# Sliding-window attention and a tanh-shrink feed-forward layer: a new order of loads in the first batch, another form of the second, and another V product in the third and fourth

## Chip, core and metric

The kernel runs on one core of a Trainium2 chip. The metric is the device time of one execution in microseconds; the time of a kernel is the median of its runs. The core has five engines, each with its own queue of instructions worked off in order: TensorE (matrix products), VectorE, ScalarE, GpSimd and SyncE. Transfers are issued from the queues of SyncE, ScalarE and GpSimd.

## What is computed

Eight batches of eight heads, 576 positions, head dimension 64. Each query attends to itself and the 63 positions before it. The attention output, 4608 tokens of 512 values, goes through a feed-forward layer with 2048 hidden values. Everything comes in and goes out as float32; the kernel works in bfloat16 with float32 accumulation.

```python
scores = scale * np.matmul(q, k.transpose(0, 1, 3, 2))
rel = pos[:, None] - pos[None, :]
scores = np.where((rel >= 0) & (rel < 64), scores, -1e9)
attn = softmax(scores)
x = (attn @ v).transpose(0, 2, 1, 3).reshape(B * S, H * D)
h = x @ w_in
out = (h - np.tanh(h)) @ w_out
```

## The kernel before

**Tiling.** Two heads (h and h + 4 of a batch) form a pair; pair g belongs to batch g // 4, so there are 32. The 576 positions are nine windows of 64. The keys of a window lie on 128 partitions (64 earlier ones and its own 64), so a score tile is 128 keys by 64 queries for each head. The feed-forward layer works on nine chunks of 512 tokens (eight windows); a chunk has 16 hidden tiles (`h`, four matmuls each, then tanh on ScalarE and the subtraction L392 on VectorE) and 16 output groups (`y`, four matmuls each; after every fourth, `y_out` copies a 128-row result out of PSUM and stores it).

**One pair of heads.** `load` brings q and k of a pair, cast to bfloat16 on the way, by a transfer issued on GpSimd; the tiles `kall` and `qall` hold a whole batch and there are two of each. Then q and k are transposed on TensorE, in one of two ways. `tr_heads` (L255) transposes straight from the loaded layout, 12 small transposes for six row groups and two heads. `cast` first rearranges on an engine to `qb` or `kb`, and `tr` (L263) then needs six; it copies q out twice, one half by ScalarE, one by VectorE (`qt`, zero-padded, both heads in one product). Scores follow, an exponential on ScalarE writes `pt`, and keys outside the window must be made nothing. This is done in two ways too. `hides` (L281) puts a large negative bias into PSUM by two matmuls ahead of the scores. Or the exponentials are multiplied on VectorE by a mask of zeros and ones (L300, L327), which lies in PSUM bank 5, written there once by `see`.

**V.** `load_v_all` brings a batch of V (`vall`, one buffer), `cast_v` rearranges it to `vb` with a column of ones, and nine transfers make the windows `vw`: `keys_v` writes the upper 64 partitions, and `shift_dve` makes the lower ones by copies on VectorE (batches 0 and 1); `windows_v` writes both by transfer (batch 2 from GpSimd, the later ones from SyncE). The product of probabilities and V carries the sum of the probabilities in the column of ones. `tile_pv` (L309) makes it with 20 matmuls of 64 columns of the array each, the two heads side by side, and normalizes by one reciprocal (L313) and one product on 128 partitions (L315). `pv` and `norm` make it with nine matmuls over both heads (L333), one reciprocal (L340) and two products on 64 partitions (L344). `x_tr` (L350) transposes the result to the tokens' chunk `xT`.

**Order.** The schedule is written out by hand. The instructions of batch 0 come first, straight in line. Then comes a list of positions h: `OPS[h]` says which hidden tile or output group TensorE does at h, and `at(h, ...)` hangs the attention work of later batches behind it. Positions 0 to 30 (even) are chunk 0's hidden tiles, 32 to 47 its output groups, 48 to 63 chunk 1's hidden tiles, 64 to 79 its output groups, and so on. Batch 1 hangs at 33 to 47, pairs 8 to 11 at 50 to 77 and pairs 12 to 15 at 68 to 94 (by `std`, whose product with V is `whole_pv`). PSUM has eight banks; the numbers in the calls are banks. In the first batch scores go to banks 0, 1 and 4, 5; hidden tiles of chunks 0 to 2 use banks 0 to 2, the output groups of chunks 0 and 1 banks 1 and 2.

**What the steps below touch.** GpSimd's queue takes its loads, V's moves and its casts in the written order. Pairs 8, 9 and 12 to 14 have their casts on VectorE, pairs 10, 11 and 15 on GpSimd. Before the change pair 10's q is cast at position 55 and its k at 56, pair 11's at 60 and 61, and the loads of pairs 12 to 15 are issued at 60 and 61.

Of the kernel before, what the change touches and what calls it, by code (L numbers as in the profile page):

```python
# [8 lines left out]
BF16 = mybir.dt.bfloat16  # L9
ALU = mybir.AluOpType  # L10
# [5 lines left out]
def kernel(  # L16
# [9 lines left out]
    nc = tc.nc  # L26
    B, H, S, D = q.shape
    NP = H // 2
# [29 lines left out]
    ident = const.tile([128, 128], BF16, name="ident")  # L58
    tick = const.tile([1, 1], BF16, name="tick")
    seen = const.tile([128, 128], BF16, name="seen")  # L60
    mask = ps[:, 5, 448:480].bitcast(BF16)
    hide = const.tile([128, 2, 64], BF16, name="hide")
    WIDE = 1024, 1024
# [17 lines left out]
    def move(eng, o, i):  # L81
        if eng is nc.scalar:
            nc.scalar.activation(o, i, ACT.Copy)  # L83
        else:
            eng.tensor_copy(o, i)  # L85

    def load(g, n, eng):

        b, pr = divmod(g, NP)
        if g == 0:  # L90
            t = qk_pool.tile([P, 2, E * D], F32, tag=n, name=n + "f")
        else:
            if (b, n) not in whole:
                whole[b, n] = all_pool.tile([P, H, E * D], BF16, tag=n, name=n + "all")
            t = whole[b, n][:, pr::NP]
        eng.dma_start(out=t, in_=(q if n == "q" else k)[b, pr::NP].rearrange("h (p e) d -> p h (e d)", e=E))  # L96
        stage[g, n] = t
# [8 lines left out]
    def pace(h):  # L106

        c, m = divmod(h // 2 - 1, M)
        nc.gpsimd.tensor_copy(tick, gT[c][0:1, m, 0:1])
# [101 lines left out]
    def make_seen():  # L211
# [2 lines left out]
        nc.gpsimd.affine_select(seen, seen, compare_op=ALU.is_ge, fill=0.0,  # L214
                                base=64, pattern=[[-1, 128]], channel_multiplier=1)

    def see():
        nc.tensor.transpose(ps[:, 5, 448:512].bitcast(BF16), seen, ident)

# [55 lines left out]

    GROUPS = (0, 5), (5, 4)

    def hides(grp, banks):
        n = GROUPS[grp][1]
        for h in range(2):  # L280
            nc.tensor.matmul(ps[:, banks[h], 0:64 * n], ident, hide[:, h].unsqueeze(1).to_broadcast([128, n, 64]),  # L281
                             start=True, stop=False)

    def tile_scores(g, grp, banks, how="hide"):

        j0, n = GROUPS[grp]
        if how == "hide":
            hides(grp, banks)
        for i in range(n):
            j = j0 + i  # L290
            for h in range(2):
                r = slice(64 * h, 64 * h + 64)
                nc.tensor.matmul(ps[:, banks[h], 64 * i:64 * i + 64], kT[g % NR][r, 64 * j:64 * j + 128],  # L293
                                 qs[g % 2][r, 64 * j:64 * j + 64], start=how == "mask", stop=how == "mask" or i == n - 1)
        o = PT[g % NPT][:, j0:j0 + n].rearrange("p j (h t) -> p h j t", h=2)
        nc.scalar.activation(o, pair_of(banks)[:, :, 0:64 * n].rearrange("p h (j t) -> p h j t", t=64),  # L296
                             ACT.Exp, scale=scale)
        if how == "mask":
            p = PT[g % NPT][:, j0:j0 + n].rearrange("p j (h t) -> p (j h) t", h=2)
            nc.vector.tensor_tensor(p, p, mask.unsqueeze(1).to_broadcast([128, 2 * n, 64]), ALU.mult)  # L300

    def tile_pv(g, banks):

# [123 lines left out]
    def at(h, fn, *args):  # L427
        items.setdefault(h, []).append((fn, args))

    def pace(h):  # L430

        c, m = [OPS[i][1:] for i in range(h) if OPS.get(i, "-")[0] == "h"][-1]
        nc.gpsimd.tensor_copy(tick, gT[c][0:1, m, 0:1])
# [13 lines left out]
    load(1, "q", G)  # L447
    make_hide()
    make_seen()
    load(2, "k", G)  # L450
    load(2, "q", G)

    warm(9)
    cast_flat(0, "q", V)
# [3 lines left out]
    see()  # L458
    for pr in range(NP):
        cast_v(0, pr, V)  # L460
    tile_scores(0, 0, (0, 1))
    tile_scores(0, 1, (4, 5))
    for j, eng in enumerate((Y, G, A, G, Y, G, G, Y, G)):
        keys_v(0, j, eng)
    for n in "kq":
        load(3, n, G)
    load_w_in(0)
    load_w_in(1)
    load_w_out(0)
# [10 lines left out]
    tile_scores(1, 0, (0, 1), "mask")  # L480
    tile_scores(1, 1, (4, 5), "mask")
    tr_heads(2, "q", 3, A)
    tile_scores(2, 0, (0, 1), "mask")
    tile_scores(2, 1, (4, 5), "mask")
    tr_heads(3, "k", 2, V)
    shift_dve(0, 0, 4)
    tile_pv(0, (6, 7))
    tr_heads(3, "q", 3, A)
    hides(0, (0, 1))
    hides(1, (4, 5))  # L490
    tile_scores(3, 0, (0, 1), "hidden")
    tile_scores(3, 1, (4, 5), "hidden")
    tile_pv(1, (6, 7))
    tile_pv(2, (2, 3))
    tile_pv(3, (0, 1))
    x_tr(0, 0, 0, 4, 4, A)
    x_tr(0, 0, 4, 9, 5, A)
    warm(2)
    x_tr(0, 1, 0, 4, 6, V)
    x_tr(0, 1, 4, 9, 3, A)  # L500

    at(33, lambda: [cast_v(1, pr, V) for pr in range(NP)])
    at(34, more_constants)
    at(35, lambda: [keys_v(1, j, G) for j in range(NJ)])
    at(35, load, 7, "q", G)
    at(35, load_v_all, 2)
    for g in 8, 9:
        at(35, load, g, "k", G)
        at(35, load, g, "q", G)
    at(39, tr_heads, 4, "k", 3, V)  # L510
    at(40, tr_heads, 4, "q", 0, A)
    at(41, tile_scores, 4, 0, (4, 5))
    at(41, tr_heads, 5, "k", 3, V)
    at(42, tile_scores, 4, 1, (4, 5))
    at(42, tr_heads, 5, "q", 0, A)
    at(43, tile_scores, 5, 0, (4, 5))
    at(43, tr_heads, 6, "k", 3, V)
    at(44, tile_scores, 5, 1, (4, 5))
    at(44, tr_heads, 6, "q", 0, A)
    at(45, tile_scores, 6, 0, (4, 5))  # L520
    at(45, shift_dve, 1, 0, 4)
    at(46, tile_scores, 6, 1, (4, 5))
    at(46, tr_heads, 7, "k", 3, V)
    at(46, tr_heads, 7, "q", 0, A)
    at(46, tile_pv, 4, (6, 7))
    at(47, tile_scores, 7, 0, (4, 5))
    at(47, tile_pv, 5, (6, 7))
    at(47, tile_scores, 7, 1, (4, 5))
    at(47, x_tr, 1, 0, 0, 4, 3, V)
    at(47, tile_pv, 6, (6, 7))  # L530
    at(47, x_tr, 1, 0, 4, 9, 0, A)
    at(47, tile_pv, 7, (4, 5))
    at(47, x_tr, 1, 1, 0, 4, 3, V)
    at(47, x_tr, 1, 1, 4, 9, 6, A)

    at(48, lambda: [cast_v(2, pr, G) for pr in range(NP)])
    at(49, lambda: [windows_v(2, j, G) for j in range(NJ)])
    for g in 10, 11:
        at(49, load, g, "k", G)
        at(49, load, g, "q", G)  # L540
    at(49, load_v_all, 3)
    for g in range(12, 16):
        at(60 + (g - 12) // 2, load, g, "k", G)
        at(60 + (g - 12) // 2, load, g, "q", G)
    for i in range(2):
        at(140 + 4 * i, more_zeros, i)

    def whole_pv(g):
        for i in range(3):
            pv(g, i)  # L550
        norm(g)

    def std(g, ck, cq, t, tk, ss, ms, p):
        at(cq, cast, g, "q", V if g not in (10, 11, 15) else G)
        at(ck, cast, g, "k", V if g not in (10, 11, 15) else G)
        at(t, tr, g, "q", 3, A, V)
        at(tk, tr, g, "k", 3, A)
        for i in range(3):
            at(ss + 2 * i, scores, g, i, 4)
        at(ms, masking, g)  # L560
        at(p, whole_pv, g)

    for i, g in enumerate(range(8, 12)):
        a = (50, 55, 60, 65)[i]
# [63 lines left out]
                    at(h, pace, h)  # L628
                    at(h, *f)

    done = None
    for h in range(32 * NC + 32):
        op = OPS.get(h)
        if op and done:
            y_out(*done)
            done = None
        if op and op[0] == "h":
            c, m = op[1:]
            if c < 2 and m == 0:
                hp_mm(c, (0, 1, 2), True)  # L640
            elif c > 1 or m > 2:
                hp_mm(c, (m,), False)
        elif op:
            yp_mm(*op[1:])
            if op[2] % 4 == 3:
                done = op[1], op[2] // 4
# [4 lines left out]
    y_out(*done)  # L651
    assert not items

# [28 lines left out]
```

The softmax here doesn't subtract the row's maximum and nothing guards it: scores larger than these inputs give would overflow.

## Time and profile before

| | us |
|---|---|
| median of 4 runs (349.55 to 351.45) | 349.84 |
| the profiled execution | 349.65 |
| its span, first to last instruction | 347.9 |
| TensorE matmul busy in the span | 319.2 (92%) |
| VectorE busy | 200.5 (58%) |
| ScalarE busy | 184.8 (53%) |
| GpSimd busy | 110.5 (32%) |

Busy times are unions of the intervals in which an engine had an instruction under way. They are averages over stages with different limits, so the stages have to be read one by one. The granted clock of TensorE is a share of full speed; its mean over the span is 0.974. The profile names the tile that an instruction writes and those that it reads ("kall<-in_k_dram" is a load of k), and the line that recorded it; L85 and L83 are the lines of `move`, through which most copies and casts go, so there the tile's name tells which copy it is. Chunk 0's hidden tiles begin at 27.4 us, its output groups at 41.9 us, chunk 1's hidden tiles at 68.5 us.

### The profile page before, as it was taken

The numbers are of one execution on the slowest core, as the hardware profiler recorded it, in microseconds if no ns is written. First come the engines' busy times: TensorE is split into PE (matmuls) and PEld (weight loads), VectorE is DVE, ScalarE is ACT, GpSimd is POOL, SyncE is SP. The second block draws the span as 40 slices with busy tenths as digits, with TensorE's granted clock in tenths as the row PEclk, the third lists the DMA queues.
The fourth block names the chain that finished last, engine by engine and source line by source line (L and its number), as shares of the span: only waits on it lengthen the run. The fifth ranks groups of instructions, "written<-read, shape, count | busy, mean of one in ns | idle before, by whom it ended". The sixth has DMA issues, their size and how long they took to land.

```text
span 347.9 us, 6234 instructions
## 1 busy us (share of the span) xinstructions
PE 319.2 (92%) x2428; PEld 175.9 (51%) x2428; DVE 200.5 (58%) x328; ACT 184.8 (53%) x335; POOL 110.5 (32%) x165
## 2 busy tenths in 40 slices
PE   6479999799988778899899999998999999999995
PEld 2364545555555444555555555554555444444442
DVE  4365833767965869576766666665666344444400
ACT  3436625478544866566566666654554444444411
POOL 8921072857902723622463363510000000000000
PEclk9559999999999999999999999999999999999999
DMA  8999999599799198347498698679821400010021
GB/s 164 148 198 215 199 171 153 79 166 152 102 178 235 37 140 143 52 94 143 99 152 164 109 168 160 107 169 200 177 73 50 110 32 30 39 53 30 30 82 71
DMA packets 51494, 42.39 MB, mean 122 GB/s; under 512 B 21080, under 2 KB 44824, under 8 KB 51464
## 3 DMA queue, kind: packets, MB, share of 16 engines
q0 software_dynamic: 21536, 20.13, 38.4%
q1 hardware_dynamic: 29648, 21.50, 25.7%
q8 instruction: 19, 0.31, 0.3%
q10 hardware_dynamic: 280, 0.36, 0.3%
q14 instruction: 11, 0.09, 0.1%
HBM read 36.70 MB, written 11.21 MB: 138 GB/s over the span
## 4 chain that ended last, share of the span: by engine, by line
PE 72%; DVE 12%; ACT 5%; DMA 4%; issue 3%; POOL 2%; SPq 2%; DVEq 0%; POOLq 0%; ACTq 0%
PE ps L404 31%; PE ps L380 29%; DVE gT L392 3%; PE ps L333 3%; PE ps L321 3%; DVE xs L344 2%; PE ps L263 2%; DVE qt L85 2%; DMA kall<-in_k_dram 2%; ACT pt L323 1%; ACT th L385 1%; SPq L160 1%; PE ps L255 1%; DMA kd<-kb 1%; ACT qt L83 1%
## 5 line engine op out<-in xcount | busy, mean ns | idle before, releaser
L380 PE MATMUL ps<-xT,wi 128*128 128x512 bf16 x576 | 144.1, 379 | 3.2 <-DVE gT L392 2.5
L392 DVE TENSOR_TENSOR gT<-ps,th 128x512 bf16<-128x512 f32 x144 | 98.7, 690 | 83.1 <-ACT th L385 81.2
L404 PE MATMUL ps<-w_out_sb,gT 128*128 128x512 bf16 x576 | 143.5, 379 | 0.0
L385 ACT ACTIVATE th<-ps 128x512 f32<-128x512 f32 x144 | 85.7, 598 | 74.0 <-PE ps L380 71.9
L380 PEld LDWEIGHTS <-wi 128*128 128x128 bf16 x576 | 61.4, 113 | 49.8 <-issue 4.1
L404 PEld LDWEIGHTS <-gT 128*128 128x128 bf16 x576 | 53.3, 98 | 54.6 <-issue 0.2
L323 ACT ACTIVATE pt<-ps 128x384 bf16<-128x384 f32 x72 | 35.3, 490 | 32.2 <-PE ps L321 31.9
L85 POOL COPY vb<-vall 72x1024 bf16<-72x1024 bf16 x24 | 24.9, 1055 | 39.6 <-DMA vall<-in_v_dram 19.7
L344 DVE TENSOR_TENSOR xs<-ps,rc 64x576 bf16<-64x576 f32 x48 | 36.2, 755 | 1.2
L409 ACT ACTIVATE ysb<-ps 128x512 f32<-128x512 f32 x36 | 21.6, 600 | 21.3 <-PE ps L404 21.3
L321 PE MATMUL ps<-qt,kt 128*128 128x128 bf16 x216 | 23.8, 219 | 3.0 <-ACT pt L323 1.4
L333 PEld LDWEIGHTS <-pt 128*128 128x128 bf16 x216 | 16.7, 98 | 14.1 <-issue 1.3
L321 PEld LDWEIGHTS <-kt 128*128 128x128 bf16 x216 | 16.3, 98 | 12.9 <-issue 2.3
L85 DVE COPY qt<-ps 64x576 bf16<-64x576 bf16 x20 | 15.2, 760 | 13.1 <-ACT qt L83 13.1
L333 PE MATMUL ps<-vw,pt 128*128 128x130 bf16 x216 | 21.4, 220 | 1.0 <-DVE xs L344 1.0
L327 DVE TENSOR_TENSOR pt<-pt,ps 128x1152 bf16<-128x1152 bf16 x24 | 17.9, 745 | 0.3 <-ACT pt L323 0.2
L85 POOL COPY qb<-qall 96x768 bf16<-96x768 bf16 x15 | 12.4, 828 | 12.9 <-DMA qall<-in_q_dram 12.9
L296 ACT ACTIVATE pt<-ps 128x640 bf16<-128x640 f32 (+1 forms) x16 | 10.2, 650 | 10.8 <-PE ps L293 10.8
L85 POOL COPY kb<-kall 96x768 bf16<-96x768 bf16 x19 | 15.8, 832 | 0.0
L85 DVE COPY kt<-ps 128x576 bf16<-128x576 bf16 x8 | 6.1, 757 | 14.6 <-PE ps L255 14.6
L83 ACT ACTIVATE kt<-ps 128x576 bf16<-128x576 bf16 x20 | 13.0, 648 | 2.3 <-PE ps L263 2.3
L96 POOL DMA_DIRECT2D qall<-in_q_dram x15 | 9.8, 656 | 12.8 <-DMA wi<-in_moe_w_in_dram 4.8
(69 smaller groups left out, 199.3 us busy)
## 6 DMA issues: line engine op xcount, KB each, us to landing
out_dram<-ysb SPq DMA_DIRECT2D x36, 256.0 KB, 2.1
vw<-vb SPq DMA_DIRECT2D x40, 130.0 KB, 4.6
vall<-in_v_dram POOLq DMA_DIRECT2D x7, 576.0 KB, 10.2
kall<-in_k_dram POOLq DMA_DIRECT2D x4, 576.0 KB, 8.5
qall<-in_q_dram POOLq DMA_DIRECT2D x4, 576.0 KB, 9.1
kall<-in_k_dram POOLq DMA_DIRECT2D x15, 144.0 KB, 7.7
qall<-in_q_dram POOLq DMA_DIRECT2D x15, 144.0 KB, 5.3
wi<-in_moe_w_in_dram POOLq DMA_DIRECT2D x2, 1024.0 KB, 12.5
```

The lines of the kernel that those rows point to most:

```text
L83: nc.scalar.activation(o, i, ACT.Copy)
L85: eng.tensor_copy(o, i)
L321: nc.tensor.matmul(sp[:, i, :], kT[g % NR][:, 64 * j:64 * j + 128], qT[g % NR][:, :, 64 * j:64 * j + 64], start=True, stop=True)
L323: nc.scalar.activation(PT[g % NPT][:, 3 * grp:3 * grp + 3, :], sp, ACT.Exp, scale=scale)
L327: nc.vector.tensor_tensor(p, p, mask.unsqueeze(1).to_broadcast([128, 2 * NJ, 64]), ALU.mult)
L333: nc.tensor.matmul(ps[:, 5 + grp, 130 * i:130 * i + 130], PT[g % NPT][:, j, :], vw[b % 2][:, j, 2 * pr:2 * pr + 2, :], start=True, stop=True)
L344: nc.vector.tensor_tensor(xo[r, :, :, pr, :], ov[r, :, :, h, 0:D], rc[r].to_broadcast([64, 3, 3, 64]), ALU.mult)
L380: nc.tensor.matmul(hp, w_in_tile(ki, m), chunk_tile(c)[:, :, ki % 2, 64 * (ki // 2):64 * (ki // 2) + 64], start=(ki == 0), stop=(ki == 3))
L385: nc.scalar.activation(th, hp, ACT.Tanh)
L392: nc.vector.tensor_tensor(gT[c][:, m, :], hp, th, ALU.subtract)
L404: nc.tensor.matmul(yp, gT[c][:, m, s * 128:(s + 1) * 128], w_out_sb[:, m, :], start=(m == 0), stop=(m == M - 1))
L409: nc.scalar.activation(ysb, ps[:, yp_bank(c, s), :], ACT.Copy)
```

## The change

**First batch.** The loads of pair 3's k and q are issued on GpSimd right after pair 2's. V's nine moves (`keys_v`) all go to GpSimd's queue behind them. The mask is copied once into SBUF (`mask_sb`), and the masks of `tile_scores` are read from there. The order of the transposes, score groups and V products is changed, and V products use more banks.

**Second batch.** q and k are cast on VectorE (`cast_pair`) and transposed six at a time (`tr_rows`); the bias products go, and masks are multiplied on VectorE. The copy-out of the last output row group of chunk 0 (`flush`) stands ahead of the attention work at position 47, and the V products take other banks. Pairs 10 and 11 are loaded at position 35, with 8 and 9.

**Third and fourth batch.** Pairs 12 to 15 are all loaded at position 50. Pairs 8 to 15 make their V product with `tile_pv`.

```diff
+    mask_sb = const.tile([128, 64], BF16, name="mask_sb")
+    def copy_mask():
+        nc.vector.tensor_copy(mask_sb, mask)
+    def tr_rows(g, which, bank, eng):
+        src = rows.pop((g, which)).rearrange("p e h d -> p e (h d)")
+        tp = ps[:, bank, :].bitcast(BF16)[:, 0:E * P].rearrange("c (e p) -> c e p", e=E)
+        for e in range(E):
+            nc.tensor.transpose(tp[:, e, :], src[:, e, :], ident[:P, :P])
+        o = qs[g % 2] if which == "q" else kT[g % NR][:, 64:]
+        move(eng, o.rearrange("c (p e) -> c p e", e=E), tp.rearrange("c e p -> c p e"))
...
-            nc.vector.tensor_tensor(p, p, mask.unsqueeze(1).to_broadcast([128, 2 * n, 64]), ALU.mult)
+            nc.vector.tensor_tensor(p, p, mask_sb.unsqueeze(1).to_broadcast([128, 2 * n, 64]), ALU.mult)
...
-    load(2, "k", G)
-    load(2, "q", G)
+    for g in 2, 3:
+        load(g, "k", G)
+        load(g, "q", G)
...
+    copy_mask()
...
-    for j, eng in enumerate((Y, G, A, G, Y, G, G, Y, G)):
-        keys_v(0, j, eng)
-    for n in "kq":
-        load(3, n, G)
+    for j in range(NJ):
+        keys_v(0, j, G)
...
     tr_heads(2, "q", 3, A)
+    tr_heads(3, "k", 2, V)
     tile_scores(2, 0, (0, 1), "mask")
     tile_scores(2, 1, (4, 5), "mask")
-    tr_heads(3, "k", 2, V)
+    tr_heads(3, "q", 3, A)
     shift_dve(0, 0, 4)
-    tile_pv(0, (6, 7))
-    tr_heads(3, "q", 3, A)
...
-    tile_pv(1, (6, 7))
-    tile_pv(2, (2, 3))
-    tile_pv(3, (0, 1))
-    x_tr(0, 0, 0, 4, 4, A)
-    x_tr(0, 0, 4, 9, 5, A)
+    tile_pv(0, (6, 7))
+    tile_pv(1, (2, 3))
+    tile_pv(2, (0, 1))
+    x_tr(0, 0, 0, 4, 6, A)
+    x_tr(0, 0, 4, 9, 7, A)
+    tile_pv(3, (4, 5))
...
-    for g in 8, 9:
+    for g in 8, 9, 10, 11:
         at(35, load, g, "k", G)
         at(35, load, g, "q", G)
-    at(39, tr_heads, 4, "k", 3, V)
-    at(40, tr_heads, 4, "q", 0, A)
-    at(41, tile_scores, 4, 0, (4, 5))
+    at(36, cast_pair, 4, V)
+    at(37, tr_rows, 4, "k", 3, V)
+    at(38, tr_rows, 4, "q", 0, A)
+    at(38, cast_pair, 5, V)
+    at(39, tile_scores, 4, 0, (4, 5), "mask")
...
+    at(44, shift_dve, 1, 0, 4)
+    at(45, tile_scores, 6, 1, (4, 5), "mask")
+    at(45, cast_pair, 7, V)
+    at(47, flush)
     at(46, tile_pv, 4, (6, 7))
+    at(46, tr_rows, 7, "k", 3, V)
+    at(46, tr_rows, 7, "q", 0, A)
     at(47, tile_pv, 5, (6, 7))
+    at(47, tile_scores, 7, 0, (4, 5), "mask")
+    at(47, tile_scores, 7, 1, (0, 3), "mask")
+    at(47, tile_pv, 6, (1, 2))
...
-    for g in 10, 11:
-        at(49, load, g, "k", G)
-        at(49, load, g, "q", G)
     at(49, load_v_all, 3)
     for g in range(12, 16):
-        at(60 + (g - 12) // 2, load, g, "k", G)
-        at(60 + (g - 12) // 2, load, g, "q", G)
+        at(50, load, g, "k", G)
+        at(50, load, g, "q", G)
...
-        at(p, whole_pv, g)
+        at(p, tile_pv, g, (6, 7))
```

More of the change, by code (lines that the diff above doesn't have):

```diff
@@ L428, in at, with flush @@
         items.setdefault(h, []).append((fn, args))
+    done = []
+    def flush():
+        if done:
+            y_out(*done.pop())
     def pace(h):
@@ L492, with cast_pair @@
     tile_scores(3, 1, (4, 5), "hidden")
-    tile_pv(1, (6, 7))
-    tile_pv(2, (2, 3))
-    tile_pv(3, (0, 1))
-    x_tr(0, 0, 0, 4, 4, A)
-    x_tr(0, 0, 4, 9, 5, A)
-    warm(2)
-    x_tr(0, 1, 0, 4, 6, V)
-    x_tr(0, 1, 4, 9, 3, A)
+    tile_pv(0, (6, 7))
[4 more added lines that the diff above has]
+    tile_pv(3, (4, 5))
+    warm(2)
+    x_tr(0, 1, 0, 4, 3, V)
+    x_tr(0, 1, 4, 9, 6, A)
+    def cast_pair(g, eng):
+        cast(g, "k", eng)
+        cast(g, "q", eng)
     at(33, lambda: [cast_v(1, pr, V) for pr in range(NP)])
@@ L506 @@
     at(35, load_v_all, 2)
-    for g in 8, 9:
+    for g in 8, 9, 10, 11:
         at(35, load, g, "k", G)
         at(35, load, g, "q", G)
-    at(39, tr_heads, 4, "k", 3, V)
-    at(40, tr_heads, 4, "q", 0, A)
-    at(41, tile_scores, 4, 0, (4, 5))
[L513 to L524, printed above, removed]
+    at(36, cast_pair, 4, V)
[3 more added lines that the diff above has]
+    at(39, tile_scores, 4, 0, (4, 5), "mask")
+    at(39, tr_rows, 5, "k", 3, V)
+    at(40, tile_scores, 4, 1, (4, 5), "mask")
+    at(40, tr_rows, 5, "q", 0, A)
+    at(40, cast_pair, 6, V)
+    at(41, tile_scores, 5, 0, (4, 5), "mask")
+    at(42, tr_rows, 6, "k", 3, V)
+    at(42, tile_scores, 5, 1, (4, 5), "mask")
+    at(43, tr_rows, 6, "q", 0, A)
+    at(44, tile_scores, 6, 0, (4, 5), "mask")
+    at(44, shift_dve, 1, 0, 4)
+    at(45, tile_scores, 6, 1, (4, 5), "mask")
+    at(45, cast_pair, 7, V)
+    at(47, flush)
     at(46, tile_pv, 4, (6, 7))
-    at(47, tile_scores, 7, 0, (4, 5))
+    at(46, tr_rows, 7, "k", 3, V)
+    at(46, tr_rows, 7, "q", 0, A)
     at(47, tile_pv, 5, (6, 7))
[L528 to L531, printed above, removed]
+    at(47, tile_scores, 7, 0, (4, 5), "mask")
+    at(47, tile_scores, 7, 1, (0, 3), "mask")
+    at(47, tile_pv, 6, (1, 2))
+    at(47, x_tr, 1, 0, 0, 4, 6, A)
+    at(47, x_tr, 1, 0, 4, 9, 7, A)
     at(47, tile_pv, 7, (4, 5))
@@ L534 @@
     at(47, x_tr, 1, 1, 4, 9, 6, A)
-    at(48, lambda: [cast_v(2, pr, G) for pr in range(NP)])
+    for pr in range(NP):
+        at(48, cast_v, 2, pr, G)
     at(49, lambda: [windows_v(2, j, G) for j in range(NJ)])
-    for g in 10, 11:
-        at(49, load, g, "k", G)
-        at(49, load, g, "q", G)
     at(49, load_v_all, 3)
     for g in range(12, 16):
-        at(60 + (g - 12) // 2, load, g, "k", G)
-        at(60 + (g - 12) // 2, load, g, "q", G)
+        at(50, load, g, "k", G)
+        at(50, load, g, "q", G)
     for i in range(2):
         at(140 + 4 * i, more_zeros, i)
[L548 to L551, printed above, removed]
     def std(g, ck, cq, t, tk, ss, ms, p):
@@ L629 @@
                     at(h, *f)
-    done = None
     for h in range(32 * NC + 32):
         op = OPS.get(h)
-        if op and done:
-            y_out(*done)
-            done = None
+        if op:
+            flush()
         if op and op[0] == "h":
@@ L645 @@
             if op[2] % 4 == 3:
-                done = op[1], op[2] // 4
+                done.append((op[1], op[2] // 4))
         for fn, args in items.pop(h, []):
@@ L650 @@
             g_sub(*op[1:])
-    y_out(*done)
+    flush()
     assert not items
```

## The prediction

> **What bounds the kernel now.** I read the page first, then busy times by stretch, then the chain of waits, then the timeline of single engines where the diff touches them. "Position" is the number h in the written order of TensorE steps; "pair" is a head pair, four to a batch.
>
> Busy time by stretch (PE, PEld, DVE, ACT, POOL busy; granted clock; DMA share; GB/s):
>
> ```profile
> 20.00:30.00 10.00, 9.54 (x144) 6.54 (x142) 4.81 (x11) 4.57 (x10) 1.23 (x2) 0.69 1.11 213
> 50.00:60.00 10.00, 10.00 (x141) 5.33 (x140) 3.01 (x5) 5.25 (x9) 4.27 (x7) 1.00 1.06 160
> 60.00:70.00 10.00, 7.63 (x165) 5.02 (x164) 6.29 (x13) 4.85 (x10) 8.16 (x12) 1.00 0.56 90
> ...
> 250.00:300.00 50.00, 50.00 (x256) 25.15 (x255) 24.87 (x38) 22.92 (x39) 0.00 (x0) 1.00 0.24 64
> ```
>
> TensorE is full from 40 to 60 us and after 140, which the diff leaves alone; whatever is gained or lost by 140 us stands at the end. DMA is full to about 62 us.
>
> The chain between 86 and 98 us (start, us, what):
>
> ```profile
> 86.05 1.29 DVE gT L392 x2
> 87.33 0.14 DVE rc L340
> 87.50 0.75 DVE xs L344
> 88.26 0.76 DVE xs L344
> ...
> 91.83 1.21 DVE qb L85
> ...
> 93.32 0.75 DVE xs L344
> 94.08 0.76 DVE xs L344
> ...
> 96.06 0.77 DVE qt L85
> ```
>
> VectorE runs without a gap here, with two normalizations (L340, L344) in it. TensorE waits for it only at the end, 0.72 us at 96.87.
>
> GpSimd's own order, between (start, us, instruction, idle before and releaser):
>
> ```profile
> 61.54 4.03 POOL L85 COPY vb<-vall 72x1024 bf16<-72x1024 bf16 x4 [7.09 <-issue]
> ...
> 66.47 4.24 POOL L160 DMA_DIRECT2D vw<-vb  x8
> 70.70 0.66 POOL L96 DMA_DIRECT2D kall<-in_k_dram  x1
> 73.11 0.65 POOL L96 DMA_DIRECT2D qall<-in_q_dram  x1 [1.75 <-DMA vw<-vb]
> ...
> 76.36 0.63 POOL L96 DMA_DIRECT2D qall<-in_q_dram  x1 [1.98 <-DMA vw<-vb]
> 76.98 0.84 POOL L145 DMA_DIRECT2D vall<-in_v_dram  x1
> 80.73 0.82 POOL L85 COPY qb<-qall 96x768 bf16<-96x768 bf16 x1 [2.90 <-DMA qall<-in_q_dram]
> 81.50 0.82 POOL L85 COPY kb<-kall 96x768 bf16<-96x768 bf16 x1
> 82.27 0.64 POOL L96 DMA_DIRECT2D kall<-in_k_dram  x1
> ```
>
> A DMA issue can hold this queue. The issues at 24.04, 29.40, 34.30 and 39.24 each waited 4.3 to 4.8 us for w_in's two and w_out's two loads, and each of these is the eighth DMA before it on the queue; 73.11 and 76.36 wait likewise. So an issue goes only when its eighth predecessor has landed. The casts of pair 10 (80.73) come ahead of pairs 12 to 15's loads (from 82.27), and TensorE transposes that q at 83.68, two us after it is ready.
>
> **First batch.** Two waits go. Scores of group 1 stood 1.27 us (13.22) and 1.29 us (16.78) behind the mask product, which reads its mask from the bank that they write; the mask in SBUF (one copy more, at most 0.43 us by the 128x512 row, while VectorE is idle) ends that. K of pair 3, issued at 12.19 and landed 5.2 us later at 17.4, is issued at 8.55 and should land at 12.5 to 13.5. Against it, all nine key moves are issued on GpSimd: 9 x 0.57 = 5.1 us from 9.9 to 15.0, where SyncE and ScalarE took four of them. The last lands at 16.5 to 19.5 (3.5 to 4.8 us each), so `shift_dve` and the first V product end at about 18.5 to 19.7 instead of 20.9, and pair 3's scores are out of the way by then. Four normalizations of 1.05 us follow, and the first chunk could start at 24 to 25.5 instead of 27.4. The weights are issued 1.5 us later, but the first landed at 23.7 as the end of a full DMA stretch; I take it unmoved (0 to +1.3). Gain: 2.3 us (0 to 3.4).
>
> **It doesn't get through whole.** V of batch 1, issued at 16.42, lands 27.0 us later at 43.42, the moment VectorE casts it; it waits for bytes, which the change doesn't lessen. Its casts (1.43 us) and two memsets (1.03 us) then stand ahead of pair 4's new casts, so the first transpose can't come before about 46.4, where TensorE would be ready at 44.8: 1.6 us are given back, 0.7 kept.
>
> **Second batch.** TensorE sheds the hide products (0.27 + 0.22 = 0.49 us a pair, four pairs: 1.95 us) and half of the transposes (12 in 0.38 us; six take 0.20 to 0.26 at L263: 0.15 x 8 = 1.2 us). VectorE takes on casts (0.50 + 0.35 us a pair: 3.4) and mask products (0.49 + 0.42: 3.6); from position 36 to 45 it then works 9.7 us (four pairs' casts 3.4, three k copies of 0.76, six masks 2.7, the shift 1.3), while TensorE needs about 11.4 (ten output groups of 0.86, six transposes of 0.22, six score groups of 0.25), so TensorE still leads. New waits: about 0.25 us for qs (ScalarE copies it behind an exponential, once hidden by the hide products), and at positions 46 and 47 about 1.7 us for the shift and pair 7's casts, which queue behind the masks. The end of the batch (position 48 done at 71.75) also loses its 1.4 us wait for V products in one bank pair and the 0.48 us wait for the output copy, which `flush` puts first. Net 2.7 us (1.5 to 3.5). Together TensorE would be 3.4 us ahead at position 48.
>
> **GpSimd's order, which takes it back.** Eight loads (pairs 12 to 15) now stand at position 50, ahead of pair 10's casts at 55, and the last of them is the eighth DMA after V's load for batch 3. So pair 10's q can't be cast until that V has landed. Step by step: V of batch 2 landed at 61.0 (50.80 + 10.2), held by bytes as above. Pair 11's q waits for it, +0.63 us, ahead of the four casts. The nine windows were issued by 70.7, and the last landed 8.6 us later at 78.8; I add 0.6 and take off 0.8 of at most 1.6 us, since an output store (256 KB at 160 GB/s) that ran among them moves ahead: 78.6. V's load follows at once, with no k or q before it; the same load took 4.3 us after pair 11's q had landed (76.36 + 5.8 = 82.1 to 76.98 + 9.5 = 86.5): 82.9. Then the held issue, 0.63, and the cast, 0.82: q of pair 10 is there at 84.4. Ends: 82.3, if V takes 2.9 us (four 144 KB loads landed 0.73 us apart) and the windows end at 77.9; 88.0, if V lands at 86.5 as before. The nearest row is the 4.3 us one. TensorE, ready at 83.68 - 3.4 = 80.3, waits 4 us and is at 84.4: 0.7 us behind the old run (-1.4 to +4.3). Loads 10 and 11, moved ahead, have 62 to 66 us to land in, where DMA was nearly idle: nothing.
>
> **Third and fourth batch.** The V product in column tiles: 20 matmuls go from 65.33 to the next transpose at 65.77, 0.44 us, against 0.51 for nine at L333; entering costs about 0.1 there (five transposes take 0.38 before the next L309, against 0.28 by cadence). So nothing for TensorE (-0.6 to +1.2 over eight pairs). The Trainium skill ("TensorEngine Tiling (Array Packing)", Key Properties) says that a change of tiling mode drains the engine. It speaks against sixteen new switches; by that rule alone each pair would be dearer, by the row it is even. The normalization falls from 0.22 + 1.52 to 0.22 + 0.82 us (L313, L315): 0.69 x 8 = 5.5 us of VectorE, of which only what TensorE waits for counts: 0.72 at 96.87, about 0.5 of the 0.82 at 109.47, 0.1 near 121, 0.69 in 136 to 140, where TensorE is busy 1.55 of 3.5 us. Sum 2.0 (0.8 to 3.2).
>
> **Sum.** The profiled run took 349.65, span 347.9. 349.65 + 0.7 - 2.0 = 348.35; the median is 0.19 above that run, so 348.5. About 0.5% either way is what a measurement of this kernel tells from no change: 348.1 and 351.6.
>
> **Rivals.** (a) GpSimd doesn't hold pair 10: V lands by 79 or the wait isn't where I put it. Then 3.4 + 2.0 come through: 344.4. For it: the loads are small; against it: four such waits of over 4 us in the first 40 us. 17%.
> (b) Slower: V's load lands as late as before, at 86.5, because the loads behind it share its engines. Pair 10's q comes at 88.0, +4.3: 352.1. From 87.4 on the kernel is slower by over 0.5%. For it: DMA is at 0.95 to 1.2 there; against it: less stands ahead of V. 20%.
> (c) The 4 us wait drops TensorE's clock. The clock was 0.50 from 10 to 26 us, and came back only after TensorE had been nearly full from 20 us; four to six us of work at half speed are 2 to 3 us: 351.0. Against it: 1.00 throughout 136 to 139.5, with 1.55 of 3.5 us busy. 18%. The skill ("TensorE: Matmul & The Clock Gate", The HAM clock gate) drops the clock after an idle window of about 3.4 us; a 4 us gap would sometimes hold one, and half of one such window, 1.7 us, would make the sum 350.2: an estimate from that page.
> (d) The forecast, held by pair 10: 348.5, its own range 346.4 to 350.7. 45%.
>
> **Numbers.** Faster: (a) and nearly half of (d), 0.38. Same: the other half of (d) and most of (c), 0.35. Slower: (b), a quarter of (c), little of (d), 0.27. Range 344.2 to 352.8: half of (a) lies below, half of (b) above.
>
> **What would show it.** No TensorE wait on L300 before 18 us; first L380 at 24 to 25.5; VectorE's V cast still at 43.4; position 48 about 3 us early; GpSimd's last load of pair 15 waiting for vall until about 83; a TensorE gap of 3 to 5 us ahead of L263 there; L315 in the third batch at 0.82. No such gap means (a). If pair 10's cast ends after 87, it is (b).

## The result, and the profile after

| | before | after |
|---|---|---|
| median, us (same chips) | 350.35 (64 runs) | 352.69 (43 runs) |
| the profiled execution, us | 349.65 | 354.06 |
| its span, us | 347.9 | 352.3 |

The changed kernel is slower: ratio 1.0061, interval 1.0046 to 1.0076. The time lies inside the predicted range; the forecast, slightly faster, had the sign wrong. (Ratios here leave disturbed executions out, so they need not equal the ratio of two medians.)

In the profile after, `move` is L84 and L86, `load` L97, tr's transposes L267, `hides` L294, `tr_rows` L287, the mask product L313, the scores of `scores` L334 and of `tile_scores` L306, `tile_pv` L322 with its normalization L326 and L328, hidden tiles L393, the subtraction L405, output groups L417.

Busy time by stretch, after, the columns as before (PE, PEld, DVE, ACT, POOL; granted clock; DMA share; GB/s):

```profile
60.00:70.00 10.00, 7.24 (x129) 5.02 (x130) 8.17 (x18) 5.33 (x11) 5.91 (x8) 1.00 0.98 178
80.00:90.00 10.00, 5.13 (x25) 2.44 (x23) 3.59 (x6) 3.72 (x7) 5.77 (x9) 0.79 1.05 156
```

The second line is new: TensorE is busy for half of ten microseconds, and the mean clock is 0.79. GpSimd's queue there, after (start, us, instruction, idle before and releaser):

```profile
63.79 0.63 POOL L97 DMA_DIRECT2D qall<-in_q_dram  x1 [4.71 <-DMA vall<-in_v_dram]
64.42 4.02 POOL L86 COPY vb<-vall 72x1024 bf16<-72x1024 bf16 x4
...
73.20 0.52 POOL L161 DMA_DIRECT2D vw<-vb  x1 [0.20 <-issue]
73.74 0.85 POOL L146 DMA_DIRECT2D vall<-in_v_dram  x1
76.64 0.65 POOL L97 DMA_DIRECT2D kall<-in_k_dram  x1 [2.05 <-DMA vw<-vb]
...
80.40 0.63 POOL L97 DMA_DIRECT2D kall<-in_k_dram  x1
85.26 0.63 POOL L97 DMA_DIRECT2D qall<-in_q_dram  x1 [4.23 <-DMA vall<-in_v_dram]
85.88 0.83 POOL L86 COPY qb<-qall 96x768 bf16<-96x768 bf16 x1
```

The hold is where the prediction put it: the last of eight loads waits for V of batch 3 (`vall`), and pair 10's cast stands behind it. And TensorE, after:

```profile
79.84 1.89 PE L393 MATMUL ps<-xT,wi 128*128 128x512 bf16 x8
81.57 0.33 PE L334 MATMUL ps<-qt,kt 128*128 128x128 bf16 x3
86.77 0.66 PE L267 MATMUL ps<-ident,qb 96*128 96x96 bf16 x6 [4.87 <-POOL qb L86]
87.23 3.61 PE L393 MATMUL ps<-xT,wi 128*128 128x512 bf16 x8
90.78 0.76 PE L322 MATMUL ps<-vw,pt 128*64 128x65 bf16 x20
```

It stands still for 4.87 us, and then eight matmuls take 3.61 us, where at full clock eight take 1.89 (the first line): the clock is 0.50 from 85.77 to 92.59. The chain of waits, after, has the transfer by name; none of these three pieces was in the old chain at this place:

```profile
73.74 11.24 DMA vall<-in_v_dram
...
85.88 0.84 POOL qb L86
...
86.77 0.66 PE ps L267 x6
```

Where the 4.4 us of span come from is read from the starts of the tanh instructions, which follow TensorE's hidden tiles one by one (after minus before; minus is earlier):

| tanh | before at | after | pair 15's loads later (below) | loads alone (below) | mask in PSUM, no hold (below) |
|---|---|---|---|---|---|
| chunk 0, first | 29.34 | -0.83 | -1.46 | +0.65 | -1.01 |
| chunk 1, first | 71.08 | -1.94 | +1.88 | +0.65 | -1.94 |
| chunk 1, 13th | 83.72 | -1.95 | +1.88 | +0.65 | -1.94 |
| chunk 1, 14th | 85.11 | +4.06 | +1.88 | +2.75 | -1.94 |
| chunk 1, 16th | 87.90 | +5.64 | +1.88 | +2.68 | -1.93 |
| chunk 3, first | 141.30 | +3.58 | -0.06 | +2.91 | -3.95 |
| last | 329.55 | +3.74 | +0.03 | +2.42 | -4.46 |

A lead of 1.94 us is won, 7.6 us are lost between 82 and 93 us, 1.9 us come back by the end. The remaining 0.7 us of the two spans lie behind the last tanh.

### The profile page after: what moved, and what is told of

Same layout as the page of the kernel before. It is cut to its first block, busy times and chain, and to the rows that moved or that the text cites. A ratio compares the mean times of both kernels' runs of the same rounds, so it can differ in the third digit from the quotient of the medians.

```text
span 352.3 us, 6289 instructions
## 1 busy us (share of the span) xinstructions
PE 322.1 (91%) x2452; PEld 175.3 (50%) x2452; DVE 200.9 (57%) x336; ACT 185.2 (53%) x336; POOL 113.4 (32%) x169
## 4 chain that ended last, share of the span: by engine, by line
PE 67%; DMA 13%; POOL 9%; DVE 4%; ACT 3%; issue 2%; SPq 0%; POOLq 0%; ACTq 0%; DVEq 0%
PE ps L417 30%; PE ps L393 26%; DMA vall<-in_v_dram 10%; PE ps L334 3%; POOL vw L176 3%; PE ps L267 3%; PE ps L346 2%; DMA kt<-kd 2%; DMA kall<-in_k_dram 1%; PE ps L322 1%; POOL vb L86 1%; POOL vw L161 1%; DVE gT L405 1%; ACT pt L336 1%; POOL vall L154 1%
## 5 line engine op out<-in xcount | busy, mean ns | idle before, releaser
L393 PE MATMUL ps<-xT,wi 128*128 128x512 bf16 x576 | 146.9, 385 | 2.6 <-DVE gT L405 2.5
L405 DVE TENSOR_TENSOR gT<-ps,th 128x512 bf16<-128x512 f32 x144 | 98.7, 690 | 84.5 <-ACT th L398 82.7
L417 PE MATMUL ps<-w_out_sb,gT 128*128 128x512 bf16 x576 | 143.8, 379 | 0.0
L393 PEld LDWEIGHTS <-wi 128*128 128x128 bf16 x576 | 62.0, 114 | 51.2 <-issue 6.7
L417 PEld LDWEIGHTS <-gT 128*128 128x128 bf16 x576 | 53.3, 98 | 53.9 <-issue 0.2
L86 POOL COPY vb<-vall 72x1024 bf16<-72x1024 bf16 x24 | 24.8, 1051 | 29.7 <-DMA vall<-in_v_dram 19.3
L86 DVE COPY qt<-ps 64x576 bf16<-64x576 bf16 x20 | 15.2, 760 | 21.6 <-ACT qt L84 21.6
L334 PE MATMUL ps<-qt,kt 128*128 128x128 bf16 x216 | 24.0, 220 | 2.9 <-ACT pt L336 1.4
L357 DVE TENSOR_TENSOR xs<-ps,rc 64x576 bf16<-64x576 f32 x32 | 24.2, 755 | 0.8
L334 PEld LDWEIGHTS <-kt 128*128 128x128 bf16 x216 | 16.2, 98 | 13.1 <-issue 2.3
L346 PEld LDWEIGHTS <-pt 128*128 128x128 bf16 x144 | 12.0, 98 | 12.5 <-issue 1.3
L346 PE MATMUL ps<-vw,pt 128*128 128x130 bf16 x144 | 16.0, 220 | 1.0 <-DVE xs L357 1.0
L86 POOL COPY qb<-qall 96x768 bf16<-96x768 bf16 x15 | 12.4, 825 | 11.0 <-DMA qall<-in_q_dram 7.0
L86 POOL COPY kb<-kall 96x768 bf16<-96x768 bf16 x19 | 15.6, 826 | 0.0
L84 ACT ACTIVATE qt<-ps 64x576 bf16<-64x576 bf16 x20 | 12.7, 635 | 5.6 <-PE ps L267 5.6
L97 POOL DMA_DIRECT2D qall<-in_q_dram x15 | 9.7, 644 | 17.4 <-DMA vall<-in_v_dram 8.9
L97 POOL DMA_DIRECT2D kall<-in_k_dram x15 | 10.1, 676 | 13.2 <-DMA w_out_sb<-in_moe_w_out_dram 5.9
L267 PE MATMUL ps<-ident,qb 96*128 96x96 bf16 x120 | 8.6, 209 | 6.0 <-POOL qb L86 4.9
```

The costliest lines, as they stand in the source:

```text
L267: nc.tensor.transpose(tp[:, e, :], src[:, e, :], ident[:P, :P])
L334: nc.tensor.matmul(sp[:, i, :], kT[g % NR][:, 64 * j:64 * j + 128], qT[g % NR][:, :, 64 * j:64 * j + 64], start=True, stop=True)
L357: nc.vector.tensor_tensor(xo[r, :, :, pr, :], ov[r, :, :, h, 0:D], rc[r].to_broadcast([64, 3, 3, 64]), ALU.mult)
L393: nc.tensor.matmul(hp, w_in_tile(ki, m), chunk_tile(c)[:, :, ki % 2, 64 * (ki // 2):64 * (ki // 2) + 64], start=(ki == 0), stop=(ki == 3))
L405: nc.vector.tensor_tensor(gT[c][:, m, :], hp, th, ALU.subtract)
L417: nc.tensor.matmul(yp, gT[c][:, m, s * 128:(s + 1) * 128], w_out_sb[:, m, :], start=(m == 0), stop=(m == M - 1))
```

## Experiments

### The hold: loads moved back, loads alone, one pair's loads moved back

**The changed kernel with the loads of pairs 12 to 15 back at positions 60 and 61:**

```diff
-        at(50, load, g, "k", G)
-        at(50, load, g, "q", G)
+        at(60 + (g - 12) // 2, load, g, "k", G)
+        at(60 + (g - 12) // 2, load, g, "q", G)
```

> The changed kernel with the loads of pairs 12 to 15 put back to positions 60 and 61, behind the casts of pairs 10 and 11. Theory H (the eight loads hold GpSimd's queue until V of batch 3 has landed, and with it pair 10's cast): the 4.9 us TensorE wait and the half clock behind it go, the 1.9 us lead at position 56 and the 2.1 us won later stay, so 345.5 to 347.5 us, 0.986 to 0.992 of the kernel before. Rival R (the loss is in the column tiles or in VectorE's new casts and masks): 351 to 353 us.

Median 350.89 us, not the 345.5 to 347.5 expected; the six executions lie from 345.05 to 355.34, too far apart for a ratio. The wait for pair 10 is gone from the profile (an execution of 350.21 us), but another took its place 20 us earlier. VectorE there:

```profile
61.99 0.82 DVE L328 TENSOR_TENSOR xs<-ps,rc 128x640 bf16<-128x640 f32 x1
62.74 5.15 DVE L313 TENSOR_TENSOR pt<-pt,mask_sb 128x640 bf16<-128x640 bf16 x2
67.81 0.21 DVE L326 RECIPROCAL rc<-ps 128x10 f32<-128x10 f32 x1
```

GpSimd, the same kernel and stretch:

```profile
63.18 4.02 POOL L86 COPY vb<-vall 72x1024 bf16<-72x1024 bf16 x4
```

Of the two mask products the first, 0.49 us elsewhere, takes 4.81 us, and it ends 0.35 us after GpSimd's four copies of V (67.2). TensorE's product with V waited 3.25 us for it, and the clock was 0.50 from 65.8 to 72.6:

```profile
67.60 0.83 PE L322 MATMUL ps<-vw,pt 128*64 128x65 bf16 x20 [3.25 <-DVE pt L313]
```

So the hold was a true fault of the changed kernel, and not the only one.

**The kernel before with the new loads alone** (pairs 10 and 11 at position 35, pairs 12 to 15 at position 50, nothing else):

```diff
-    for g in 8, 9:
+    for g in 8, 9, 10, 11:
...
-        at(60 + (g - 12) // 2, load, g, "k", G)
-        at(60 + (g - 12) // 2, load, g, "q", G)
+        at(50, load, g, "k", G)
+        at(50, load, g, "q", G)
```

> The kernel before with nothing but the changed load positions (pairs 10 and 11 at 35, pairs 12 to 15 at 50). Theory H: pair 10's q is cast at about 86, where TensorE wants it at 83.7; a wait of 2 to 3 us, too short for the clock to fall in most runs, and nothing won elsewhere: 351.5 to 353.5 us. Rival R: 350 to 350.7, no change.

353.28 us, ratio 1.0047 (1.0012 to 1.0082). GpSimd in this kernel:

```profile
79.89 0.63 POOL L96 DMA_DIRECT2D kall<-in_k_dram  x1
85.02 0.63 POOL L96 DMA_DIRECT2D qall<-in_q_dram  x1 [4.50 <-DMA vall<-in_v_dram]
85.64 0.83 POOL L85 COPY qb<-qall 96x768 bf16<-96x768 bf16 x1
```

The order of loads makes the hold by itself, and costs 1.6 us (0.4 to 2.9) by itself. It costs less than in the changed kernel because TensorE comes later to the same wait: it loses 2.1 us at the 14th tanh, where the changed kernel, 2.6 us ahead of this one, loses 6.0 (a part of it at the halved clock, which this kernel's profile has not). V landed at nearly the same time in both (84.73 and 84.98), so a lead in front of it is worth nothing.

**Pair 15's two loads alone moved behind pair 10's casts**, in the changed kernel with its masks read from PSUM (the masks are below):

```diff
-        at(50, load, g, "k", G)
-        at(50, load, g, "q", G)
+        at(50 if g < 15 else 60, load, g, "k", G)
+        at(50 if g < 15 else 60, load, g, "q", G)
```

> The kernel after with the mask read from PSUM bank 6 (so that no product stands still beside GpSimd) and the two loads of pair 15 at position 60; pairs 12 to 14 stay at position 50, ahead of pair 10's casts. Theory H in its sharp form (an issue goes when the eighth DMA before it on GpSimd's queue has landed): the last load ahead of pair 10's casts is then q of pair 14, whose eighth predecessor is the last window and not V of batch 3; pair 10's q is cast by 82 us, TensorE waits for less than 1.5 us there, and the end comes 3 to 4.5 us earlier than the kernel before: 346 to 347.5, ratio 0.987 to 0.992. Rival (it is the number of loads, or their bytes beside V's load, that holds the queue): six of eight loads still stand ahead, so pair 10's q is cast after 84.5 us and TensorE waits 3 us or more: 350.5 to 352.5.

348.89 us, ratio 0.9922 (0.9886 to 0.9957). GpSimd:

```profile
78.00 0.63 POOL L97 DMA_DIRECT2D kall<-in_k_dram  x1
78.63 0.63 POOL L97 DMA_DIRECT2D qall<-in_q_dram  x1
79.25 0.84 POOL L86 COPY qb<-qall 96x768 bf16<-96x768 bf16 x1
80.02 0.83 POOL L86 COPY kb<-kall 96x768 bf16<-96x768 bf16 x1
80.79 0.64 POOL L97 DMA_DIRECT2D kall<-in_k_dram  x1
```

The median is 1.4 us above what was expected, but the place is as expected: six loads stand ahead of the cast and the last of them doesn't wait, although V landed as late as 84.08. With eight, on the same chip and the same masks, the ratio is 1.0121 (below): two load instructions in another place are 0.020 of the time, some 7 us (4 to 10 by the ends of the two intervals). That is the eighth predecessor: q of pair 15 has V's load in that place, q of pair 14 a window. The number of loads, or their bytes beside V's, would still have held the cast with six of eight in place. The trace of the changed kernel also shows where the eight comes from: the transfers issued on GpSimd take eight semaphores in turn (numbers 99 to 106), and the held load waits for number 102, which V's load took eight transfers before. So the wait is one that this program's semaphores make; no run shows a limit of the queue itself. The lead that this profile has lost at chunk 1 (+1.88) went earlier: its clock was 0.50 from 48.3 to 51.7 and from 68.8 to 72.2 us.

### The halved clock: the wait filled

Twenty matmuls of 512 columns that feed nothing, put in TensorE's queue ahead of pair 10's transposes in the changed kernel:

```diff
+    at(60, warm, 20)
```

> The changed kernel with 20 matmuls of 512 columns, whose result is not used, ahead of pair 10's transposes at position 60 (4.3 us of work inside the 4.9 us wait). If the wait drops the clock and this costs 2 to 3 us (theory C), it is 349.5 to 351 us with a clock of 1.00 throughout 85 to 95 us. If the clock has no share, 352.5 to 353.5.

353.36 us, ratio 1.008 (1.0047 to 1.0114). Its busy time by stretch:

```profile
80.00:90.00 10.00, 9.17 (x71) 4.65 (x69) 3.72 (x6) 4.25 (x8) 6.40 (x10) 1.00 1.08 156
```

The clock stays at 1.00 from 31 us to the end, and the kernel is no faster than without the filler. In its profile TensorE is 3.67 us behind at the 14th tanh (V landed at 85.7) and 2.90 at the last: only 0.8 us come back, where the changed kernel got 1.9 back from its 5.64. So part of what the halved clock costs at 92 us would have been lost later anyway. By the two profiles some 1.5 us of clock remain (5.64 less 3.09 of late q is 2.55 us; 1.1 us of that come back); the two medians show none of it. But the filler lasts 4.48 us, nearly as long as the wait that it fills, so in an execution in which q comes earlier it would be on TensorE's path itself; no run separates the two. The clock's share of the median stays open between 0 and 1.5 us.

### The mask in SBUF, and copies beside GpSimd

**Casts of pairs 10 and 11 moved from GpSimd to VectorE**, so that the held queue no longer stands ahead of them:

```diff
-        at(cq, cast, g, "q", V if g not in (10, 11, 15) else G)
-        at(ck, cast, g, "k", V if g not in (10, 11, 15) else G)
+        at(cq, cast, g, "q", V if g != 15 else G)
+        at(ck, cast, g, "k", V if g != 15 else G)
```

> The changed kernel, loads where they are, but the casts of pairs 10 and 11 on VectorE instead of GpSimd. Theory H: q and k of pair 10 land by 69, so no wait at position 60; VectorE gets four casts of 0.35 us more where it is full: 345.5 to 348 us. If loads that early hurt by the bytes they move and not by GpSimd's order (rival B), it stays at 351 to 353.

Median 350.03 us of six executions from 346.12 to 359.01. The ratio, 0.9888 (0.9834 to 0.9942), rests on the three at 346.1 to 347.0, where they should lie without the hold. The profile caught the slowest execution, and VectorE in it shows why it was slow:

```profile
63.21 4.95 DVE L313 TENSOR_TENSOR pt<-pt,mask_sb 128x640 bf16<-128x640 bf16 x2
...
84.70 4.48 DVE L86 COPY kb<-kall 96x768 bf16<-96x768 bf16 x1
```

The second is a copy from SBUF to SBUF that takes 0.34 us elsewhere; GpSimd copied V from 84.95 to 88.97 beside it. The first line is two products again, of which one takes 4.47 us. Copy and product end 0.2 to 0.3 us after the four copies of V beside them.

**The masks read from PSUM again** (bank 6, written by a second transpose), with the loads at 60 and 61 as in the first experiment:

```diff
-    mask_sb = const.tile([128, 64], BF16, name="mask_sb")
+    mask_sb = ps[:, 6, 448:480].bitcast(BF16)
...
+        nc.tensor.transpose(ps[:, 6, 448:512].bitcast(BF16), seen, ident)
...
-    copy_mask()
```

> The kernel of e1_loads60 (loads of pairs 12 to 15 at 60 and 61) with the masks of the first two batches read from PSUM (bank 6) instead of SBUF. In e1_loads60 one mask product took about 4.4 us instead of 0.45, while GpSimd's four copies of V ran (4.0 us). Theory P (a VectorE product with both inputs in SBUF stands still while GpSimd copies in SBUF; with one input in PSUM it doesn't): no L313 over 0.6 us, chunk 1's first tanh at 68 to 70 us, 344.5 to 347 us in nearly all runs. Rival (the product waited for something else, a landing or a semaphore): the long product comes again and the time stays at 350 to 351.

348.6 us, ratio 0.9888 (0.9834 to 0.9943), the lowest median of these runs. Its six executions lie from 345.84 to 364.31 us, and the profile is of the one at 345.84. VectorE at the same place:

```profile
62.66 0.82 DVE L329 TENSOR_TENSOR xs<-ps,rc 128x640 bf16<-128x640 f32 x1
63.40 0.90 DVE L314 TENSOR_TENSOR pt<-pt,ps 128x640 bf16<-128x640 bf16 x2
64.44 0.22 DVE L327 RECIPROCAL rc<-ps 128x10 f32<-128x10 f32 x1
```

GpSimd, the same kernel and stretch:

```profile
63.83 4.02 POOL L86 COPY vb<-vall 72x1024 bf16<-72x1024 bf16 x4
```

The second product ran beside these copies; it took its usual time, and so did four normalizing instructions, which read PSUM too. In the three other kernels with masks in PSUM the products met GpSimd's copies as well, and none took over 0.49 us. The last column of the table is this profile. These rows bear out a line of the Trainium skill ("GPSIMD Engine Reference", Specifications): GpSimd's way to SBUF is shared with VectorE, and instructions with two SBUF inputs contend. Here a product beside the four copies took about ten times its usual time, in two profiles.

**The same masks, and the loads as changed**, so that the hold stays:

> The kernel after with nothing changed but the mask: read from PSUM bank 6 instead of SBUF. Theory (in the changed kernel a mask product that stands still beside GpSimd's copies costs nothing at the end, since pair 10's q comes at the same time after it, so two faults do not add): same time as the kernel after, 352 to 353.5, ratio to the kernel before 1.003 to 1.009; the gap of 4 to 6 us ahead of pair 10's transposes stays. Rival (the mask in SBUF costs by itself in the changed kernel): 1 to 3 us less, 349.5 to 351.

355.16 us, ratio 1.0121 (1.0073 to 1.0169). The gap stays (the last load waits 3.75 us, pair 10's q is cast at 86.7), and PSUM masks win nothing behind it. That the median is 2.5 us above the changed kernel's was not expected, and its cause is open: its profile of 353.65 us is not slower than that one's. In the changed kernel's own profile, V of batch 2 landed at 63.51 and GpSimd's copies began at 64.42, after the two mask products (63.39, 0.91 us). In three profiles with the mask in SBUF, V landed at 61.57 to 62.96, and one product or both were held, by 0.7 to 4.3 us each. Whether the two meet depends on when V lands, and that lay anywhere from 60.98 to 64.56 in the fourteen profiles.

### The parts one at a time

**Column tiles alone** (before, with `tile_pv` for pairs 8 to 15):

```diff
-        at(p, whole_pv, g)
+        at(p, tile_pv, g, (6, 7))
```

> The kernel before with nothing but the V products of pairs 8 to 15 in column tiles. My sum says 2.0 us won (0.8 to 3.2): 347.2 to 349.5. Rival (changes of tiling mode cost TensorE 0.15 us or more a pair, or VectorE isn't what it waits for): 350.3 to 352.

348.96 us, ratio 0.9927 (0.9901 to 0.9953): 2.6 us won (1.6 to 3.5). The chain of waits near 95 us reads:

```profile
92.87 1.95 DVE qb L85
...
94.85 0.23 DVE rc L313
...
95.11 0.82 DVE xs L315
95.93 0.26 DVE kb L85
96.19 0.66 DVE pt L327
...
96.89 0.77 DVE qt L85
```

One normalizing product of 0.82 us stands where two of 0.75 stood. The cast of q ahead of them takes 1.95 us, where 0.35 is usual; GpSimd's copies of V run beside it. The profiled execution, 350.34 us, is the longest of the twelve.

**The second batch alone** (before, with casts on VectorE, `tr_rows`, masks in SBUF and `flush`):

> The kernel before with nothing but the second batch's part (casts on VectorE, six transposes, masks from SBUF, other banks, output copy first). My sum says 2.7 us won, 347 to 348.5. Theory P says that the last masks or casts of the batch meet GpSimd's V copies, which start at about 61.5 here, and stand still for up to 4 us: then 349.5 to 352, with one L313 or one copy of pairs 7 to 9 over 2 us.

350.97 us, ratio 1.0012 (0.9981 to 1.0042): nothing won that the runs can tell. VectorE in the profile (349.75 us) shows one reason:

```profile
63.36 2.33 DVE L313 TENSOR_TENSOR pt<-pt,mask_sb 128x640 bf16<-128x640 bf16 x2
```

The products again run beside GpSimd's copies of V, which began at 62.13, and the clock was 0.50 from 66.3 to 73.2: 0.36 us late at the end of chunk 0 became 1.24 at the first tanh of chunk 1. In six profiles without the stall and the halved clock, the changed kernel's among them, the same part won 0.9 to 2.3 us over that stretch.

**The first batch alone:**

```diff
+    copy_mask()
...
-    for j, eng in enumerate((Y, G, A, G, Y, G, G, Y, G)):
-        keys_v(0, j, eng)
...
+    for j in range(NJ):
+        keys_v(0, j, G)
...
```

> The kernel before, with the first batch's part of the change alone (loads of pair 3 early, V's nine moves on GpSimd, the mask in SBUF, the new order); second to fourth batch as before. Theory G (the first batch's gain is given back where the second batch waits for V's load, which lands at 43 to 45 us whatever the first batch does): chunk 0 starts 1 to 2 us earlier, but from position 48 on TensorE is no more than 0.8 us ahead; time -0.7 to +0.3 us against the kernel before, ratio 0.998 to 1.001. Rival (the first batch's gain goes through and it is the second batch's part that is worth nothing): 1.5 to 2 us ahead at position 48 and at the end, ratio 0.994 to 0.996.

350.57 us, ratio 0.9998 (0.9969 to 1.0027). Its profile is 0.12 us early at the first tanh of chunk 0 and still 0.12 at that of chunk 1, V of batch 1 having landed at 45.39; from chunk 2 to chunk 5 it is 0.95 early, and then it loses 2.7 us behind a wait of 2.13 us for a transfer of k (238.85) and at a halved clock (0.50 from 240.0 to 243.4). Alone, the first batch's new order is worth nothing that the runs can tell.

**V's key moves back on three queues**, in the changed kernel:

```diff
-    for j in range(NJ):
-        keys_v(0, j, G)
+    for j, eng in enumerate((Y, G, A, G, Y, G, G, Y, G)):
+        keys_v(0, j, eng)
```

> The changed kernel with V's nine key moves of the first batch spread over SyncE, GpSimd and ScalarE as in the kernel before; all else changed. If the 5 us of issues on GpSimd push everything behind them in its queue (w_in's first half landed at 25.4 instead of 23.7, V of batch 2 at 63.5 instead of 61.0), then w_in is back at 23.5 to 24.3, V of batch 3 lands 1 to 2.5 us earlier than 85.0, pair 10's q is cast by 84.3 to 85.7, and the kernel takes 350 to 351.7 us. If the late V has another cause, 352.3 to 353.3.

353.35 us, ratio 1.0042 (1.0007 to 1.0077), as the changed kernel. V of batches 2 and 3 landed no earlier (64.56 and 85.52), so the moves do not make V late.

### Nine more fillers

The best kernel with filler matmuls in the tail of the second batch, where TensorE was busy for 7.5 of 10 us:

```diff
+    at(47, warm, 4, 1)
...
+    at(47, warm, 5, 0)
```

> The changed kernel with the loads of pairs 12 to 15 at positions 60 and 61, the mask in PSUM bank 6, and nine more filler products of 512 columns in the second batch's tail, which feed nothing (four ahead of pair 6's V product, five ahead of the last transposes). Theory K (the clock falls to 0.50 at about 66 us in some executions since TensorE is busy only 7.2 of 10 us between 60 and 70): no stretch at 0.50 after 30 us, runs closer together, 345.5 to 347, ratio 0.986 to 0.990. Rival (the clock has nothing to do with the spread of the runs, or the fillers stand on the path): 347.5 to 349, spread as without them.

349.6 us, ratio 0.9966 (0.9936 to 0.9996), executions from 348.01 to 351.57. The fillers show no gain: apart from its one execution of 364.31 us, the kernel without them lies as close together (within 3.6 us) and about a lower median. Its profile has no halved clock at 66 us, but one from 238.4 to 241.9, behind a wait of TensorE for a transfer of k; the kernel before with the first batch's part has the same one. TensorE was 2.0 us ahead at chunk 3 and lost 3.3 between 210 and 247 us.

## Why the prediction was wrong, step by step

**The mechanism was right, its size was not.** The hold, the instruction that waits, what it waits for and the cast that stands behind it are as predicted, and taking it away shows it. The step that failed is "pair 10's q is there at 84.4". It came at 86.7:

- The last window, issued at 73.20, landed at 79.0, where 78.6 was worked out: +0.4.
- V landed 6.0 us behind it, at 84.98, where the prediction took 4.3 and named 82.9: +1.7. The row behind the 4.3 was the wrong row. It ran from the landing of pair 11's q (82.1) to that of V (86.5); but in that trace V's packets already ran from about 80 us on, beside the last loads ahead of it. From first packets to landing V took about 6.5 us there, and about 8.5 in the changed kernel, where windows ran beside it up to 79 us. The two transfers overlapped, so the difference of two landings was less than the second one's own time. In the six profiles with all eight loads at position 50 V landed at 84.04 to 85.66, never at 82.9.
- The held load was issued at 85.26, 0.28 us after V's landing, which had no term: +0.3.

But for rounding the sum is the 2.3 us, so TensorE was 3.1 us behind the old run at pair 10's transposes, and not 0.7.

**The halved clock** was a rival at 18%, priced at 2.5 us, and stood in the sum at nothing. The 4.87 us wait did halve it for 6.8 us, and TensorE fell a further 2.55 us behind in the profile. The mechanism and the price at that place were right. That it reaches the end in full was not shown: with the wait filled, the median did not fall (the filler itself may have cost time).

**Position 48, "3.4 us ahead"**, was 1.94. First hidden tiles began at 25.45, inside "24 to 25.5", but their first seven matmuls took 2.80 us, where eight take 1.89 at full clock, so the tanh was 0.83 early. V of batch 1 landed at 44.42 and not 43.42, and the first transpose came at 47.48 (the prediction: not before 46.4):

```profile
44.51 1.55 DVE L86 COPY vb<-vall 72x1024 bf16<-72x1024 bf16 x4 [1.89 <-DMA vall<-in_v_dram]
...
47.14 0.29 DVE L86 COPY kb<-kall 96x768 bf16<-96x768 bf16 x1
```

The second batch won 1.1 us in place of 2.7 (the terms written down for it add up to 3.1). None of that moved the end, because the hold takes any lead.

**"V of batch 2 landed at 61.0"** was one profile's value used as the kernel's. It varies by 3.6 us between profiles, and decides whether VectorE and GpSimd meet. The mask in SBUF was costed at one copy; nothing in the prediction asked who else uses SBUF, though the old profile had a copy of 1.21 us (`qb`, at 91.83) beside GpSimd's copies.

**Third and fourth batch, 2.0 us**, was right in size, 1.9 in the profile from its largest lag and 2.6 (1.6 to 3.5) alone, but partly by luck. Its largest term, 0.72, was TensorE's wait at 96.87, put down to VectorE's normalizations. In the kernel with the first batch alone, which keeps these normalizations, TensorE has no wait there, and VectorE's cast of q is short:

```profile
91.71 0.39 DVE L86 COPY qb<-qall 96x768 bf16<-96x768 bf16 x1
```

In the old profile this cast took 1.21 us (91.83) and ended 0.22 us behind GpSimd's copies of V, so the wait belongs, at least in part, to the stall that also held the mask products; the normalizations alone don't make it. The term of 0.69 for 136 to 140 us is borne out: from 134 to 141 us each of the ten profiles with column tiles gains 0.76 or 0.77, the three without them nothing.

**Sum.** For the profiled execution: +3.1 (late q) + 2.55 (clock) - 1.9 (tail) = +3.7 at the last tanh, where the prediction had +0.7 - 2.0 = -1.3. That what is lost by 140 us stands at the end held here (+3.58 at 141 us), but not in two other profiles, which lost 2.7 and 3.3 us behind 210 us. Rival (a), no hold, was priced at 344.4 for a kernel whose old run takes 349.84; the kernel without hold and with masks in PSUM gives 0.9888 of that, 345.9 (344.0 to 347.8), so the price is not contradicted. The 1.5 us between the two would fit the smaller lead (1.94 for 3.4), but the runs don't resolve it. Rival (b), V at 86.5, was half right: V came later than forecast but not as late as before. Its cause, that the loads behind share V's engines, shows in the packets: from 80 to 84 us V's 1024-byte packets fall from 112 to 62 a microsecond while the loads' 768-byte ones rise from 9 to 180, and before, with no load behind yet, V had 146 a microsecond at 82. It wasn't tried by a run: in every kernel some loads follow V closely.

## What to carry to other kernels

Before moving issues ahead of a cast on one queue, ask which earlier transfer each of them waits for (here the eighth before it) and when that one lands: here one pair of loads on the wrong side of the cast was worth some 7 us. Take a transfer's duration from its first packets to its landing, not from the landing before, and look at several executions before a landing is used as a fixed time. When work moves to VectorE or its operands to SBUF, look for what GpSimd copies at that moment; an operand left in PSUM avoided the stall.

## Not expected of the hardware

- A VectorE product of two SBUF operands (0.49 us) took 4.81 us beside four GpSimd copies in a row, a VectorE copy from SBUF to SBUF (0.34 us) 4.48 us; each ended 0.2 to 0.35 us behind the last of the four. With one operand in PSUM the product took its usual time beside the same copies. The copy of 1.19 us in the changed kernel (67.47) is the same stall with less of it left: it began 0.97 us before GpSimd's last copy ended and ended 0.22 behind it. But in the kernel with the second batch alone the two products took 1.15 and 1.26 us and were done while GpSimd's copies still ran. What lets VectorE in between two copies is open.
- The halved clock put TensorE 2.55 us behind in one profile, and a kernel that kept it at 1.00 through the same wait was not faster by its median. Nor does it take a standstill: between 30 and 330 us the clock fell eleven times in these fourteen profiles, and in the 3.4 us before each, TensorE had been busy for between none and 51% of the time.
